# The causal mask moved into PSUM, and the last transform folded twice, in a gated mix of attention and a spectral filter

## The chip, the cores and the metric

The kernel runs on one core of a Trainium2 chip. The metric is the device time of one execution in microseconds. The profiles show one execution each: TensorE (PE, with its weight loads as PEld), VectorE (DVE), ScalarE (ACT), GpSimd (POOL) and the DMA queue of SyncE (SPq).

## What is computed

Input x has 2048 tokens of width 640, in bf16. The output is `g * a + (1 - g) * b`, where g is a sigmoid of one number per token.

```python
# a: attention in 4 segments of 512 tokens, 32 heads of 20
logits = einsum('bhqd,bhkd->bhqk', qs, ks) * scale + mask   # causal inside the segment
a_dot = einsum('bhqk,bhkd->bhqd', softmax(logits), vs)
a_mem = (phi(qs) @ M) / (phi(qs) @ z + 1e-6)                # memory of the segments before
o = gh * a_mem + (1 - gh) * a_dot                           # gh: one gate a head
M, z = M + phi(ks).T @ vs, z + sum(phi(ks))
a = o @ wo
# b: a filter in the frequencies of tokens and width
b = irfft2(rfft2(x) * (w_r + 1j * w_i))
```

## The kernel before, in words

**An order by hand.** The kernel records some 2200 operations, each with the buffers that it reads and writes, and `schedule` (L113) emits them in the order of a list written out in the source, `ORDER` (L741). Each number of that list names an operation and, by its last bit, one of the engines that may run it: a copy out of PSUM goes to ACT or DVE, an addition in SBUF to DVE or POOL. Every engine and SyncE's DMA queue work their share in that order, so an operation can wait for a buffer while those behind it wait too.

**Tile modes of TensorE.** A product with a `tile_position` uses a part of the array, and parts work side by side. The code numbers the modes: 0 is the whole array, 1 the score products (four groups of 32 rows, one for each of four heads, by 64 or 128 columns), 2 four strips of 32 columns, 4 two strips of 64 columns. The order decides how often the mode changes. Nearly all products are issued from L548 in `mms` (L532); the strips into which a projection of the output is cut are issued from L546. Copies out of PSUM are L557 (ACT) and L559 (DVE).

**Attention.** Heads go in 8 groups of four. `project` (L1129) makes q and k, transposed, and v for one segment. `token_order` (L1173) reads the keys' tokens in another order than the queries', with two products of 256 columns for each product of a k tile, and `v_part` (L1327) makes the odd v tiles with their halves swapped, in two strips of 64 columns. `qk_unit` (L1470) fills four PSUM banks with the scores of a unit, one bank for each of the four heads, and ACT takes the exponential into `ex` (L1508). Only the blocks on and under the diagonal are computed, and the 64-wide halves of the diagonal blocks are packed. A unit of kind 0 or 1 has 512 columns in each bank; kind 2 holds the 128 columns that are left of a group, for two groups together (256 columns in each bank). The list `PIECES` (L608) says what lies where. All units use the same four banks, so the next one begins when the exponential has read the last. In the last segment the pieces lie differently in `ex`, and kinds 1 and 2 take two exponentials each.

After the exponential, `masks` and `mask` (L1517, L1533) put zeros above the diagonal: four masks for each group, each either on POOL (selects at L1540 and L1549) or on DVE (a minimum with a table in `hm`, L1539 and L1545). Then `pv_flipped` (L1407) multiplies with v in four strips of 32 columns (five pieces of 512, 64, 320, 256 and 128 columns for each head), or, in the last segment, `pv_group` (L1556) uses the scores as weights on the whole array, ten products of 21 columns for each head.

**The filter.** `fft` (L1632) goes through F1 (over 128 token residues), D (over the width), T and the multiplication with W (L1696, DVE), Tb back, and Db, the back transform over the width: for each of 16 residues n2 and for the cosine and the sine part it adds three products of 321 columns, and ACT or DVE copies the sum to `G`. Db can begin when all of Tb is done.

**The end.** `finish_tile` (L1773) makes the output in 16 tiles of 128 tokens, in two halves of 320 columns. Fb multiplies G with the gated table `fbg` (for the right half's sine part with its negative `fbn`, made at L1249): for the cosine and the sine part each a product of 320 columns in four strips, the right half reading G backwards. Five projection products with wo are added in the same bank, the result is copied to `ot` and stored. The buffers of this stage (`gbc`, `fbg`, `ot`, `oU`, `mT`, `fbn`, `gw3`) lie over those of T and W, and `after_mid` (L968) makes each of them wait for all of these.

Of the kernel before, what the change touches and what calls it, by code (L numbers as in the profile page):

```python
# [322 lines left out]
def make_tables():  # L323
# [34 lines left out]
    ang = 2 * pi * kd[:, None] * kd[None] / D  # L358
    order = np.concatenate([od, [KD], ev])
    inv = np.zeros((2, 384, 322))  # L360
    for n_, (t, zero) in enumerate(((np.cos(ang), ()), (np.sin(ang), (0, 320)))):
        t = ck[:, None] * t
        t[list(zero)] = 0
        inv[n_, :322, :KD] = np.concatenate([t, np.zeros((1, KD))])[order]
    inv[1, :, 320] = 0
    inv = inv.reshape(6, 128, 322).transpose(1, 0, 2).reshape(128, 6 * 322)
# [32 lines left out]
    fcat = np.concatenate([F, np.eye(128), Fp], 1)  # L399
# [5 lines left out]
    p, c = np.arange(128)[:, None], np.arange(64)[None]  # L405
    q = p % 64
    keep = [np.where(t, 3.38e38, 0.0) for t in ((c >= q) & (p >= 64), (c >= q) & (p < 64), (c >= q) | (p < 64), (c >= q) | (p >= 64))]
    m = np.arange(128)[None]
    spread = [1.0 * ((p % 4 == t) & (p // 4 == m // 4)) for t in range(4)]
    hmask = np.concatenate([hmask.reshape(128, 880)] + keep + spread, 1)  # L410
# [80 lines left out]
KPOS = (0, 256, 128, 384)  # L491
VPIECES = ((0, 0, 512, 0), (1, 512, 64, 128), (1, 896, 320, 192), (2, 640, 256, 256), (3, 1216, 128, 384))
# [3 lines left out]
class Kern:  # L496
# [79 lines left out]
    def dma(self, dst, src, nbytes, r, w, prio, tr=False, name="", after=(), queue="sp"):  # L576
        def f(e):
# [3 lines left out]
            with self.nc.allow_non_contiguous_dma(reason="small strided loads"):  # L581
# [9 lines left out]
        "ld_fcat": (400.0, 350.0, 16), "ld_g": (400.0, 1500.0, 16), "ld_gc": (580.0, 200.0, 16), "ld_gw": (420.0, 600.0, 16),  # L591
# [6 lines left out]
        ("xT", 393216): (1400.0, 2600.0, 16), ("xT", 655360): (2950.0, 2100.0, 16)}  # L598
# [8 lines left out]
    UNITS = (((0,), 0), ((0,), 1), ((1,), 0), ((0, 1), 2), ((1,), 1))  # L607
    PIECES = (((0, 0, 0, 0, 0, 512), (1, 64, 64, 128, 0, 64), (0, 64, 64, 64, 64, 448)),  # L608
# [278 lines left out]
    def alloc(self):  # L887
# [25 lines left out]
        def TL(name, shape, dtype=BF):  # L913

            t = T(name, shape, dtype, at=late[0])
            late[0] += (shape[1] * mybir.dt.size(dtype) + 63) // 64 * 64
            assert late[0] <= self.cur
            return t
# [956 lines left out]
```

## Time and profile before

| | |
|---|---|
| median of three runs | 242.66 us (242.34 to 242.94) |
| the profiled execution | 242.17 us, of which the span of its instructions is 240.4 us |
| granted TensorE clock | 1.00 |
| masks on POOL | 110 instructions, 56.2 us |
| DMA | 43.46 MB, 73.9% of the engines' time in the main queue |

Matmuls are pipelined and the end of one is modelled, so TensorE's pace is read from the starts of two neighbours, not from a mean duration. A timeline row gives start, length, engine, line, operation, shapes and a count; neighbours of a like form are merged in one row. A group row ends in busy microseconds and the mean nanoseconds of one.

### The profile page before, as it was taken

The page shows a single profiled execution, that of the slowest core. Times are in us where ns is not written, and L with a number is a line of the kernel's source. Part 1 is how long each engine was busy: PE and PEld are TensorE (multiplying, and loading weights), DVE is VectorE, ACT ScalarE, POOL GpSimd, SP SyncE. Part 2 cuts the span into 40 slices and gives each one's busy share as a digit, 9 for nine tenths or more (in the row PEclk, how much of TensorE's full clock was granted, in tenths as well). Part 3 has the DMA queues.
Part 4 walks back from the last instruction along what each step waited for, and adds up shares of the span by engine and source line. Part 5 has one row for each costly group of instructions (what it writes and reads, how often), then busy time and mean ns, then how long its engine had stood idle before and what let it go on. Part 6 is the DMA issues. An engine that isn't in the chain of part 4 may idle for free.

```text
span 240.4 us, 10161 instructions
## 1 busy us (share of the span) xinstructions
PE 228.9 (95%) x4361; PEld 146.3 (61%) x4361; DVE 203.8 (85%) x493; ACT 202.7 (84%) x253; POOL 92.9 (39%) x172
## 2 busy tenths in 40 slices
PE   7999799999999999999989999999999999999993
PEld 4666367666556674654656555565555667667883
DVE  0978888999999899999999999899999679747742
ACT  2398979999999999999999999899899977678630
POOL 5203415503655407250516733504546232272810
PEclk9999999999999999999999999999999999999999
DMA  7998988678979989849986748378759862782213
GB/s 195 373 182 264 198 270 176 148 239 211 213 146 241 221 215 226 200 136 154 216 246 162 229 129 223 92 197 201 197 154 223 209 151 79 105 90 92 77 43 108
DMA packets 58072, 43.46 MB, mean 181 GB/s; under 512 B 27628, under 2 KB 55724, under 8 KB 58028
## 3 DMA queue, kind: packets, MB, share of 16 engines
q1 hardware_dynamic: 57500, 42.46, 73.9%
q8 instruction: 34, 0.56, 1.0%
q10 hardware_dynamic: 528, 0.36, 0.5%
q14 instruction: 10, 0.08, 0.1%
HBM read 22.73 MB, written 12.20 MB: 145 GB/s over the span
## 4 chain that ended last, share of the span: by engine, by line
PE 60%; DVE 15%; ACT 12%; DMA 6%; SPq 3%; issue 3%; DVEq 0%
PE psum L548 53%; ACT ex L1508 9%; PE psum L546 7%; DMA hm<-tab_hmask 3%; DMA qk_scr<-qu 2%; SPq L582 2%; DMA u_scr<-ub 2%; DVE mem L1389 1%; DVE G L559 1%; DVE oU L1791 1%; DVE ub L559 1%; DVE ex L1545 1%; DVE Pt L1696 1%; ACT qu L557 1%; DVE dn L1381 1%
## 5 line engine op out<-in xcount | busy, mean ns | idle before, releaser
L1508 ACT ACTIVATE ex<-psum 128x2048 bf16<-128x2048 f32 (+4 forms) x92 | 138.6, 1507 | 12.2 <-PE psum L548 10.7
L1549 POOL TENSOR_SCALAR_AFFINE_SELECT ex<-ex 64x256 bf16<-64x256 bf16 x66 | 26.8, 427 | 64.3 <-ACT ex L1508 63.5
L1540 POOL TENSOR_SCALAR_AFFINE_SELECT ex<-ex 128x512 bf16<-128x512 bf16 x44 | 29.4, 678 | 31.7 <-DVE ex L1545 20.3
L548 PE MATMUL psum<-qkp 20*64 20x64 bf16 (+5 forms) x1024 | 31.4, 266 | 1.6 <-ACT ex L1508 0.9
L548 PE MATMUL psum<-wv,xT 128*64 128x320 bf16 (+3 forms) x240 | 26.6, 302 | 2.4 <-DMA wv<-in_A_wv_dram 1.5
L548 PE MATMUL psum<-xT,wk 128*128 128x256 bf16 (+1 forms) x280 | 28.3, 273 | 0.0
L548 PE MATMUL psum<-xT,wq 128*128 128x512 bf16 (+1 forms) x135 | 27.9, 380 | 0.0
L1696 DVE TENSOR_TENSOR Pt<-psum,Wt 128x644 bf16<-128x644 f32 x32 | 25.8, 820 | 1.4 <-PE psum L548 1.1
L548 PEld LDWEIGHTS psum<-xT,wk 128*128 128x128 bf16 (+1 forms) x280 | 20.9, 98 | 4.4 <-issue 0.4
L548 PEld LDWEIGHTS psum<-qkp 20*64 20x64 bf16 (+1 forms) x1024 | 12.1, 100 | 18.1 <-ACT ex L1508 10.9
L546 PE MATMUL psum<-wo,oU 128*32 128x320 bf16 x480 | 21.0, 299 | 0.0
L548 PEld LDWEIGHTS psum<-wv,xT 128*64 128x64 bf16 (+1 forms) x240 | 14.8, 105 | 9.4 <-DMA wv<-in_A_wv_dram 1.7
L559 DVE CAST ot<-psum 128x320 bf16<-128x320 f32 x20 | 9.4, 489 | 10.3 <-PE psum L546 4.5
L548 PE MATMUL psum<-ex,va 128*32 128x512 bf16 (+4 forms) x480 | 17.3, 274 | 0.1
L548 PE MATMUL psum<-big,Cp 128*128 128x321 bf16 (+1 forms) x96 | 16.7, 302 | 0.7 <-DVE rs L1587 0.3
L548 PE MATMUL psum<-tt,Pt 128*128 128x128 bf16 (+1 forms) x192 | 16.4, 221 | 0.0
L1298 ACT ACTIVATE et<-qu 128x512 bf16<-128x512 bf16 x25 | 15.6, 629 | 0.4 <-DVE phk L1311 0.4
L546 PEld LDWEIGHTS psum<-wo,oU 128*32 128x32 bf16 x480 | 12.8, 97 | 3.8 <-issue 0.6
L548 PE MATMUL psum<-big,Ac 128*32 128x160 bf16 (+2 forms) x384 | 14.4, 259 | 0.7 <-DVE mem L1385 0.5
L1545 DVE TENSOR_TENSOR ex<-ex,hm 128x512 bf16<-128x512 bf16 (+1 forms) x31 | 13.8, 453 | 1.3 <-ACT ex L1508 1.0
L548 PEld LDWEIGHTS psum<-tt,Pt 128*128 128x128 bf16 (+1 forms) x192 | 12.1, 102 | 4.4 <-issue 0.9
L548 PEld LDWEIGHTS psum<-xT,wq 128*128 128x128 bf16 (+1 forms) x135 | 9.2, 97 | 8.5 <-issue 1.8
(114 smaller groups left out, 420.6 us busy)
## 6 DMA issues: line engine op xcount, KB each, us to landing
qkp<-qk_scr SPq DMA_DIRECT2D x28, 160.0 KB
qk_scr<-qu SPq DMA_DIRECT2D x12, 256.0 KB, 3.6
tt<-tab_tt SPq DMA_DIRECT2D x8, 384.0 KB, 4.4
u_scr<-ub SPq DMA_DIRECT2D x12, 256.0 KB, 3.6
Wt<-Wt SPq DMA_DIRECT2D x8, 321.0 KB, 4.0
xsb<-in_A_x_dram SPq DMA_DIRECT2D x8, 320.0 KB, 5.4
oU<-u_scr SPq DMA_DIRECT2D x15, 128.0 KB, 3.2
out_dram<-ot SPq DMA_DIRECT2D x12, 160.0 KB
```

The source lines that it names most:

```text
L546: h = e.matmul(dst, wt, r_, start=st, stop=sp_, **{**kw, "tile_position": (0, q), "skip_group_check": True})
L548: h = e.matmul(o_, l_, r_, start=st, stop=sp_, **kw)
L557: alts["act"] = (lambda e: e.activation(dst(), src(), ACT.Copy), 65 + 0.833 * n, 110.0)
L559: alts["dve"] = (lambda e: e.tensor_copy(dst(), src()), 67 + 1.04 * n, 68.0)
L582: return e.dma_start(d_, s_)
L1298: self.one("act", lambda e: e.activation(et.ap(0, [1, L]), qsl(), ACT.Exp), L, [qb], [b("et", pi_)], late, fix=94, name="phi_exp")
L1381: self.one("dve", lambda e: e.reciprocal(dn.ap(32, [1, 32]), dn.ap(0, [1, 32])), 32, [b("dn", i % 2, q) for q in range(2)], [rb], prio, fi ...
L1508: self.one("act", lambda e, d=d, q=q: e.activation(self.ex.ap(*d), self.ps(bank, *q), ACT.Exp, scale=SC), n, [bank], [self.exb(s, 2 * pr + ...
L1540: pick = lambda e: e.affine_select(ex(), ex(), [[0, 4], [1, P]], ALU.is_ge, 0.0, base=0, channel_multiplier=-1)
L1545: least = lambda e: e.tensor_tensor(dst(), src(), self.hm.ap(880 + 64 * t, [0, 4], [0, 2], [1, 64], np_=nd), ALU.min)
L1549: h = e.affine_select(self.ex.ap(e0 + d, [1280, 4], [1, 64], p0=hp, np_=np_), self.ex.ap(e0 + q, [1280, 4], [1, 64], p0=hp, np_=np_), [[0, ...
L1696: self.one("dve", lambda e, x=x, Pt=Pt, Wt=Wt, wo_=wo_, bank=bank: e.tensor_tensor(Pt.ap(x * 644, [322, 2], [161, 2], [1, 161]), self.ps(b ...
```

## The change

- **Scores.** q and k have the same token order. Small products are added into the scores' PSUM after the score products of a unit: weights are a 32-row table U (values -1 and -2^-50), the moving side is a table V (32 rows, 64 columns, values 2^64 and 2^14, read again for each block), so that a large negative number stands above the diagonal before the exponential. A unit of kind 0 gets 8 such products (for each head 64 columns on PSUM partitions 0 to 63 and 128 on 64 to 127), a unit of kind 1 gets 4 (128 columns), a unit of kind 2 gets 8 (256 columns on the first 64 partitions and 512 on the others). All masks go, on POOL and DVE.
- **Units of kind 2** hold four groups (512 columns in each bank) and have a buffer `exc` of their own, used by all groups in turn. Every exponential has 128x2048, in the last segment too: 72 in place of 92.
- **v.** The odd tiles are made on the whole array. New half-zeroed copies `vz` of v, made by `v_half` (16 copies on DVE or POOL for the four segments), serve the packed diagonal halves. `pv_flipped` has eight pieces (three more of 64 columns), the columns together as before; `pv_group` has two products of 64 weight columns, side by side, for each one of 128.
- **Back transform over d.** Odd and even frequencies are kept apart and only d from 0 to 160 is computed: products of 322, 161 and 161 columns in place of three of 321. The cosine part is copied to f32 (`eo`), the sum and the difference with the sine part are made from PSUM (`sum_Db`, 32 on DVE), and two folds for each n2 make the rows of G (`fold_Db`: 21 on POOL, 11 on DVE by the new list). Fb reads 161 and 159 columns where it read 320 and 320, and `fbn` is gone.
- **Homes.** The late buffers lie over other tiles and each waits, once, for the tile that it lies on (`once` in place of `after_mid`).
- **Tables.** `fcat` grows from 64 KB (without the identity) to 128 KB and is loaded earlier, sixth in SyncE's list; the first score unit needs it. `big` and `hm` shrink. The q and k rows of the middle tile are stored with one DMA in place of two.
- **Order.** `ORDER` and `ENDED` are written anew, with 2084 operations in place of 2232.

```diff
-KPOS = (0, 256, 128, 384)
-VPIECES = ((0, 0, 512, 0), (1, 512, 64, 128), (1, 896, 320, 192), (2, 640, 256, 256), (3, 1216, 128, 384))
+KPOS = (0, 128, 256, 384)
+VPIECES = ((4, 0, 64, 0), (0, 64, 448, 64), (5, 0, 64, 128), (1, 832, 320, 192), (2, 640, 192, 320), (6, 576, 64, 256), (7, 576, 64, 384), (3, 512, 64, 448))
...
+    CAUSAL = (((64, 0, 0, 1, 64), (64, 64, 0, 2, 64)),
+              ((0, 0, 0, 2, 192),),
+              ((64, 64, 0, 8, 64), (64, 0, 64, 4, 128)))
...
+        for u0, p0, o, n, step in self.CAUSAL[kind]:
+            for hh in range(4):
+                def th(hh=hh, u0=u0, p0=p0, o=o, n=n, step=step):
+                    return (self.ps(bank, hh * 512 + o, [step, n], [1, 64], p0=p0, np_=m), self.fcat.ap(256 + u0, [1, m], p0=32 * hh, np_=32),
+                            self.fcat.ap(448, [0, n], [1, 64], p0=32 * hh, np_=32), False, True, {"tile_position": (32 * hh, p0), "skip_group_check": True})
...
-        if u == 3:
-            self.masks(s, 2 * pr, prio)
-        elif u == 4:
-            self.masks(s, 2 * pr + 1, prio)
...
+                        for q in (0, 2):
+                            def th(i=i, hh=hh, jj=jj, q=q, bank=bank):
+                                w, v = weights(hh, 4 * i + q, jj)
+                                return (self.ps(bank, i * 88 + hh * VW, [1, DH + 1], p0=32 * q, np_=64), w,
...
+                        kc, n, o, c0 = ((P, 161, 0, 161), (P, 322, 161, 0), (66, 161, 483, 0))[c]
...
+                for q in range(2):
+                    self.one("dve", lambda e, q=q, bank=bank, eo=eo, uv=uv: e.tensor_tensor(
+                        uv.ap(322 * q, [1, 322]), eo.ap(0, [1, 322]), self.ps(bank, 0, [1, 322]), ALU.subtract if q else ALU.add),
...
-                        rows = self.G.ap(o + 322 * n_ + 320 * hf, [1 - 2 * hf, 320])
-                        wt = (self.fbn[s % 3] if hf and n_ else fb).ap(32 * (4 * a + q), [1, 32])
+                        rows = self.G.ap(o + (0, 322)[hf], [1, 161]) if n_ == 0 else self.G.ap(o + (483, 161)[hf] + 159, [-1, 159])
```

More of the change, by code (lines that the diff above doesn't have):

```diff
@@ L1391, in mem_read_tile @@
                     dn.ap(32 + 16 * q, [1, 16], [0, DH]), ALU.mult)
-            self.one("dve", fn, 320, [bank, rb], [b("mem", i, q)], prio, name="mem_mul", after=[b("xf", 2)] if s == 1 else ())
+            self.one("dve", fn, 320, [bank, rb], [b("mem", i, q)], prio, name="mem_mul", after=[b("q0", 8 + x) for x in range(2)] if s == 1 else ())
     def attend(self, s):
@@ L1482, in qk_unit, with th @@
             rb += [b("qp", pidx, j, gl) for j in range(4)] + [b("kp", pidx, j, gl) for j in range(4)]
[L1483 removed]
+            for j, kc, p0, q0, o, n in self.PIECES[kind]:
+                first = p0 not in begun
+                begun.add(p0)
                 for hh in range(4):
[L1485 to L1486 removed]
+                    def th(hh=hh, j=j, kc=kc, p0=p0, q0=q0, o=o + n_ * width, n=n, gl=gl, pad=pad, first=first):
```

350 lines of the change are left out of this document (175 added, 175 removed), and 487 rows, old and new, of tables (ENDED, ORDER, PIECES).

## The prediction, made blind

> **What bounds the kernel now.** I read the page's busy times first, then the windows, the chain, and TensorE's timeline.
>
> ```profile
> PE 228.9 (95%) x4361; PEld 146.3 (61%) x4361; DVE 203.8 (85%) x493; ACT 202.7 (84%) x253; POOL 92.9 (39%) x172
> ...
> PE 60%; DVE 15%; ACT 12%; DMA 6%; SPq 3%; issue 3%; DVEq 0%
> ```
> ```profile
> 40.00:160.00 120.00, 117.32 (x2122) 71.60 (x2115) 113.70 (x269) 115.53 (x136) 49.87 (x100) 1.00 0.80 191
> 160.00:207.00 47.00, 44.94 (x948) 28.16 (x945) 42.22 (x113) 41.11 (x52) 18.56 (x30) 1.00 0.70 169
> 207.00:240.40 33.40, 29.83 (x880) 23.27 (x878) 18.87 (x42) 18.12 (x23) 11.70 (x20) 1.00 0.40 85
> ```
>
> The columns of a window are TensorE, weight loads, VectorE, ScalarE, GpSimd, clock, DMA. From 40 to 160 us three engines are full at once: TensorE 98%, VectorE 95%, ScalarE 96%. Behind 160 TensorE stays at 93% while the other two thin out; GpSimd is never near full. The chain that ended last runs on TensorE for 60% of the span. So a saving on TensorE counts nearly in full, and one on another engine counts where TensorE waits for it. The sum below is TensorE's, against the profiled execution of 242.17 us (span 240.4); it lies 0.49 under the median of the runs.
>
> **Prices on TensorE**, from starts of neighbours in its timeline:
>
> ```profile
> 78.02 0.72 PE L548 MATMUL psum<-ex,va 128*32 128x512 bf16 x20
> 78.67 0.31 PE L548 MATMUL psum<-Bt,tt 128*128 128x322 bf16 x1
> 78.81 1.25 PE L548 MATMUL psum<-xT,wk 128*128 128x256 bf16 x10
> ...
> 80.00 0.47 PE L548 MATMUL psum<-big,Ac 128*32 128x322 bf16 x12
> ...
> 86.25 0.40 PE L548 MATMUL psum<-qkp 20*128 20x192 bf16 x8
> 86.57 0.41 PE L548 MATMUL psum<-tt,Pt 128*66 128x128 bf16 x4
> ...
> 88.68 0.32 PE L548 MATMUL psum<-qkp 20*64 20x64 bf16 x24
> 88.93 1.56 PE L548 MATMUL psum<-wv,xT 128*64 128x321 bf16 x20
> ...
> 92.46 1.24 PE L548 MATMUL psum<-xT,wq 128*128 128x512 bf16 x5
> 93.54 0.30 PE L548 MATMUL psum<-Bt,tt 128*128 128x322 bf16 x1
> 93.77 0.43 PE L548 MATMUL psum<-qkp 20*64 20x512 bf16 x12
> 94.13 0.72 PE L548 MATMUL psum<-wv,xT 128*128 128x321 bf16 x4
> ```
> ```profile
> 188.57 0.32 PE L548 MATMUL psum<-G,fbg 128*32 128x320 bf16 x4
> 188.72 0.31 PE L548 MATMUL psum<-G,fbn 128*32 128x320 bf16 x4
> 188.85 0.45 PE L548 MATMUL psum<-G,fbg 128*32 128x320 bf16 x8
> ...
> 191.12 1.16 PE L548 MATMUL psum<-va,ex 128*128 128x21 bf16 x40
> 192.21 0.32 PE L546 MATMUL psum<-wo,oU 128*32 128x320 bf16 x4
> ```
>
> *A column*: five products of 512 start at 92.46 and the next at 93.54, so 0.216 us each, 0.42 ns a column. *A change of tile mode*: a product of 322 columns takes 0.14 us in front of one of its own mode (78.67 to 78.81) and 0.23 in front of a score unit (93.54 to 93.77), so 0.09; a kind-1 unit takes 0.32 (86.25 to 86.57) for 512 columns in each of its tiles, so 0.11 on leaving. I take 0.10. *Side by side*: the kind-2 unit has 24 products, 2048 columns together; one behind the other these are 0.86 us, and the next product starts after 0.25, a mode change in it. So the tiles do run beside each other, and what counts is the longest tile's columns. The four products of Fb (188.57 to 188.72 to 188.85) take 0.14 us together, the pace of one.
>
> **The terms**, in us of TensorE.
>
> *Db*: per part 644 columns in place of 963, 319 x 0.42 ns = 0.134, 32 parts: -4.3. *Fb*: 320 columns in place of 640 for each of 32 halves, again 0.134: -4.3. Both are streamed on the whole array or in four strips, where the rows above hold the pace, so the bounds are narrow (-3.5 to -4.4 each).
>
> *Mode changes*: walking down TensorE's share of the two lists, neighbours differ in mode 238 times before and 211 times after (fewer score units, no odd v tiles in strips): 27 x 0.10 = -2.7; -2.4 to -3.0.
>
> *The mask's products*: a kind-0 or kind-1 unit gets 128 more columns in its longest tile, 0.054 us; 64 such units, +3.4. Kind 2: the longest tile has 512 score and 512 mask columns, once for four groups, where two units of 256 stood: 512 x 0.42 ns = 0.215 more, 8 times, +1.7. Together +5.1. Products with 32 rows and such a repeated moving side stand nowhere in the trace. The lower bound is 4, if part of it falls into time that a unit loses at its edges; the upper, if nothing ran side by side, is 8192 columns, 3.4 us, for each of 8 times four groups, so 27. The kind-2 row is the nearest thing, with the same tiles, and it is far on the cheap side.
>
> *PV*: 20 products took 0.65 us, less a mode change 0.55, for 1280 columns (0.53): five steps cost 0.02 beyond their columns. Three more steps in 24 groups: +0.3; nothing to +1.5. *PV of the last segment*: 40 products in 192.21 - 191.12 - 0.10 = 0.99 us, 25 ns each. Afterwards each is a pair with half the weights in two strips. If the strips work side by side a pair costs what one did; if not, twice: 0 to +8. I take +0.6, near the cheap end because of the kind-2 row, whose 24 weight loads of 64 columns fit into 0.25 us. *Keys' projection*: ten products of 256 columns take 1.19 us (78.81 to 80.00) with a mode change, so 0.109 each and 0.218 a pair, against 0.216 for one of 512: 100 pairs, -0.3. v's odd tiles keep their columns: 0.
>
> Sum: -4.3 - 4.3 - 2.7 + 5.1 + 0.3 + 0.6 - 0.3 = -5.6.
>
> [...]
>
> **The other engines** must not become the bound.
>
> ```profile
> L1508 ACT ACTIVATE ex<-psum 128x2048 bf16<-128x2048 f32 (+4 forms) x92 | 138.6, 1507 | 12.2 <-PE psum L548 10.7
> L1549 POOL TENSOR_SCALAR_AFFINE_SELECT ex<-ex 64x256 bf16<-64x256 bf16 x66 | 26.8, 427 | 64.3 <-ACT ex L1508 63.5
> L1540 POOL TENSOR_SCALAR_AFFINE_SELECT ex<-ex 128x512 bf16<-128x512 bf16 x44 | 29.4, 678 | 31.7 <-DVE ex L1545 20.3
> ```
> ```profile
> L1508 ACT ACTIVATE ex<-psum 128x2048 bf16<-128x2048 f32 x56 | 105.2, 1878 | 6.9 <-PE psum L548 6.2
> ...
> L1539 DVE TENSOR_TENSOR ex<-ex,hm 128x512 bf16<-128x512 bf16 x20 | 10.7, 544 | 2.0 <-ACT ex L1508 1.9
> ...
> L559 DVE CAST G<-psum 128x321 bf16<-128x321 f32 x18 | 8.4, 485 | 0.3 <-PE psum L548 0.3
> ...
> L1545 DVE TENSOR_TENSOR ex<-ex,hm 128x512 bf16<-128x512 bf16 x19 | 8.0, 422 | 1.3 <-ACT ex L1508 1.0 <-DMA hm<-tab_hmask 0.3
> ...
> L1385 DVE TENSOR_TENSOR mem<-psum,dn 128x320 bf16<-128x320 f32 x16 | 7.2, 484 | 0.2
> ...
> L1545 DVE TENSOR_TENSOR ex<-ex,hm 64x512 bf16<-64x512 bf16 x12 | 6.0, 503 | 0.0
> ...
> L1597 POOL TENSOR_TENSOR on<-on,mem 128x320 bf16<-128x320 bf16 x6 | 4.8, 808 | 6.9 <-DVE on L1592 6.9
> ```
>
> ScalarE: 72 x 1.878 = 135.2 in place of 138.6, and by the lists 94 copies in place of 105, at about 0.5 each: -9. VectorE: masks -24.7 (10.7 + 8.0 + 6.0); 150 copies in place of 155, -2.5; 32 `sum_Db` of 322 f32 from PSUM, near L1385's 0.484, +15.5; 11 folds, between 0.42 and 0.48 by the rows of two SBUF inputs, +5; 12 `v_half`, no dearer than these, +4; so about -3, and -1 to -6 with the small ones. GpSimd: masks -56, 21 folds at some 0.8 to 1, +19. All loads fall. But VectorE's relief lies ahead of 160 us, and the sums and folds lie in the stage of Db, where it had 42.2 of 47 us; there it loses 7.3 of masks (the third busy time of the row below, which is the same stretch for the instructions on `ex` alone) and, with 8 copies fewer, 4, and gains 20.
>
> ```profile
> 160.00:207.00 47.00, 7.71 (x240) 6.07 (x240) 7.33 (x19) 33.06 (x28) 10.61 (x21) 1.00 0.70 169
> ```
>
> The new list spreads Db further out, beside Fb and the projection, so that TensorE has work while VectorE sums; that is the cover, and without it the stage would wait for VectorE (rival 2).
>
> *Waits.* `exc` is one buffer for all groups: the kind-2 exponential waits for PV of the four groups before, and ScalarE's next copies stand behind it. The new list puts those PVs right ahead of that score unit; I cost it at nothing, at most half a microsecond, seven times. `vz` is single too: `v_half` waits for the last PV of the segment before and VectorE's copies stand behind it; nothing, to +1. The table for the mask's products is 128 KB and moved past eight loads in SyncE's list; the first score unit now needs it, and the x and weight loads stand behind it: nothing, as TensorE projects until then, to +1. The late loads wait for one tile each and can only start earlier.
>
> The forecast is 242.17 - 5.6 = **236.6 us**; its own range, with the narrow bounds and the waits, 233.5 to 239.8.
>
> **Rivals.**
>
> 1. *The waits shrink too.* ScalarE idled 10.7 us ahead of exponentials for scores and TensorE waited in turn; with 20 exponentials fewer and no masks between exponential and PV, some 5 us of that may go: 231 to 232. For it: three engines full from 40 to 160. Against: all units still share four banks, so score and exponential alternate as before. 0.17.
>
> 2. *VectorE becomes the bound in the stage of Db, slower than before.* Place: from the last Tb to the last G. The added sums and folds are 20 us there at the prices above, and a fold on GpSimd beside one on VectorE can lengthen both.
>
> ```profile
> 214.89 1.73 DVE L1539 TENSOR_TENSOR ex<-ex,hm 128x512 bf16<-128x512 bf16 x1 [1.95 <-ACT ex L1508]
> ```
>
> This minimum, 0.544 on average, took 1.73 while GpSimd selected. If a sum or a fold costs 0.8 in place of 0.48, 43 of them add 14 us, of which the spread list hides perhaps half; +7 leaves 243.6, and up to 247. It decides from about 0.75 a piece, where the stage eats the 5.6. Against: sums read one side from PSUM, like L1385, which is steady. 0.12. [...]
>
> 3. *Half-width weights double the last PV.* +8 in place of +0.6, on TensorE behind 190 us, where it is the bound: 244. It decides from a pair of about 44 ns, where the gain is gone.
>
> ```profile
> L548 PEld LDWEIGHTS psum<-va,ex 128*128 128x128 bf16 x320 | 8.8, 96 | 1.0 <-DVE ot L559 0.3 <-issue 0.3
> ...
> L548 PEld LDWEIGHTS psum<-wv,xT 128*64 128x64 bf16 x160 | 8.1, 109 | 3.8 <-DVE qu L559 0.8 <-issue 0.7 <-ACT et L1298 0.3
> ```
>
> For it: a load of half the columns is shown as longer, 109 ns against 96, and it never stood before so few moving columns. Against: the kind-2 row. 0.06.
>
> 4. *The gain goes into new waits* for `exc`, `vz` or the late loads (+3 to +5.5, all bounds at once): 240 to 242.2. 0.10.
>
> **Numbers.** Forecast 0.55, rivals 0.17, 0.12, 0.06, 0.10. About 0.3% is what a measurement of this kernel can tell from none, here 241.9 to 243.4. Faster: 0.55 + 0.17 + most of rival 4, 0.08 = 0.80; same: the rest of it and a little of 2 and 3, 0.05; slower 0.15. The range takes in rival 1 and rival 4 and leaves out most of 2 and 3: 230.5 to 242.5.
>
> **What would show it.** TensorE: Db's products in steps of 0.07 and 0.14, four of Fb in 0.07; a kind-1 unit 0.37 to its follower, a kind-2 unit 0.55; 80 products of the last PV in about 1.05. Group rows: exponentials x72 near 1878 ns, sums near 485, GpSimd under 60 us. By the windows the work up to the last Tb ends about where it did (mask +3.3, mode changes -2.8 there), and the gain appears behind it. Wrong would be: mask products behind one another (a kind-1 unit of 0.5 or more), or VectorE full from the last Tb on with TensorE waiting for `sum_Db`.

## The result and the profile after

The changed kernel takes **267.2 us** (four runs, 263.0 to 270.7) where the kernel before takes 242.56 (242.3 to 242.9): slower by a factor of 1.087 (95% interval 1.082 to 1.093). That factor goes by the two fast runs of the change, 263.0 and 264.6, and the profiled run is one of the two slow ones. I had forecast 236.6 and a range up to 242.5.

The page of the profiled execution (269.83 us, span 268.0): busy times, the granted clock in 40 slices, the queue that brings TensorE's instructions, the chain.

```profile
PE 238.0 (89%) x5304; PEld 150.0 (56%) x5325; DVE 200.2 (75%) x480; ACT 195.5 (73%) x214; POOL 64.6 (24%) x91
...
PEclk9999999995999999999999999986999658979979
...
q8 instruction: 42, 0.69, 1.1%
...
PE 54%; DMA 19%; DVE 11%; issue 5%; ACT 5%; SPq 3%; POOL 1%; DVEq 0%
```

VectorE, ScalarE and GpSimd have less to do, as forecast, yet TensorE is busy for 89% of a longer span (95% before), the clock falls to 0.5 in places, and DMA holds 19% of the chain (6% before). The waits of TensorE, first of the kernel before, then of the change (total, times, longest):

```profile
PE psum L548 <- DMA wv<-in_A_wv_dram: 1.5, 1, 1.5
...
PE psum L548 <- issue: 0.4, 1, 0.4
```
```profile
PE psum L553 <- issue: 7.8, 9, 2.1
PE psum L553 <- DVE qu L564: 5.9, 4, 3.2
PE psum L553 <- DVE mem L1400: 2.3, 1, 2.3
```

"issue" is a wait for which the profile names no releaser. One of the nine is a wait for data all the same:

```profile
99.03 0.70 SPq L587 DMA_DIRECT2D qkp<-qk_scr  x1
...
105.12 0.40 PE L553 MATMUL psum<-qkp 20*128 20x192 bf16 x8 [2.10 <-issue]
```

TensorE's sequencer stands from 102.65 to 105.07 at the semaphore of that load of score operands, and the last part of the load lands at 105.03. The same wait, of 1.6 to 2.5 us, stands at 100 to 107 us in the traces of runs 1 to 3, 9 to 12, 14 and 16. Without it the waits with no releaser come to 5.7 us in the change.

**The account.** From the profiled executions: the time in which a product or a weight load of TensorE is on record (busy), the rest (idle), and the busy time that lies in stretches at half clock, of which half is taken off to get the work at full clock.

| us | span | idle | busy at half clock | work at full clock |
|---|---|---|---|---|
| before | 240.4 | 11.4 | 0 | 229.1 |
| change | 268.0 | 29.2 | 32.4 | 222.7 |
| difference | +27.6 | +17.8 | +16.2 for its half | -6.4 |

So the work did shrink. Everything else is waits and clock. The last column is rough, since the ends of products are modelled: runs 9 and 14, with the same products as the change, come out at 227.8 and 224.8. And the clock's part differs between executions: by their mean granted clocks (0.936 here; 0.961, 0.949 and 0.948) half clock takes 17 us of this one and 10 to 14 us of the other three.

**The work's prices.** TensorE's timeline of the change: eight products of Fb, a unit of kind 1 with its mask, then the last segment's PV.

```profile
204.91 0.32 PE L553 MATMUL psum<-G,fbg 128*32 128x161 bf16 x8
205.06 0.85 PE L551 MATMUL psum<-wo,oU 128*32 128x320 bf16 x20
...
206.18 0.40 PE L553 MATMUL psum<-qkp 20*128 20x192 bf16 x8
206.41 0.23 PE L553 MATMUL psum<-fcat 32*128 32x128 bf16 x4
206.56 0.20 PE L553 MATMUL psum<-vz,ex 128*64 128x21 bf16 x1
...
207.90 0.17 PE L553 MATMUL psum<-va,ex 128*64 128x21 bf16 x1 [0.41 <-issue]
210.19 0.23 PE L553 MATMUL psum<-va,ex 128*64 128x21 bf16 x3 [2.11 <-issue]
```
```profile
96.73 0.71 PE L553 MATMUL psum<-qkp 20*64 20x64 bf16 x64
97.25 0.40 PE L553 MATMUL psum<-fcat 32*64 32x512 bf16 x8
97.59 0.31 PE L553 MATMUL psum<-Bt,tt 128*128 128x322 bf16 x1
```

Eight products of Fb take 0.15 (0.07 for four), the kind-1 unit 0.38 to its follower: as forecast. The kind-2 unit takes 0.86, not 0.55. And between 207.90 and 210.19 TensorE stands for 2.1 us in the middle of one PV, at a product that waits for no semaphore.

**The clock.** Windows of 3.41 us, in pairs: one that ends where the clock drops, and the one after (length, busy us and count of TensorE, loads, VectorE, ScalarE, GpSimd, clock, DMA).

```profile
25.53:28.94 3.41, 1.68 (x29) 0.80 (x29) 1.13 (x3) 2.84 (x3) 0.06 (x1) 1.00 0.41 106
56.25:59.66 3.41, 1.30 (x41) 0.95 (x39) 0.00 (x0) 2.08 (x4) 0.00 (x0) 1.00 1.21 219
59.66:63.07 3.41, 2.29 (x104) 1.59 (x104) 2.76 (x9) 0.60 (x1) 0.74 (x3) 0.50 0.86 100
175.71:179.13 3.42, 1.07 (x24) 0.57 (x25) 1.30 (x5) 1.62 (x1) 1.16 (x2) 1.00 0.84 204
179.13:182.54 3.41, 3.08 (x77) 1.89 (x65) 2.94 (x10) 1.85 (x2) 1.70 (x3) 0.50 1.09 240
206.43:209.85 3.42, 1.23 (x60) 0.97 (x50) 1.82 (x5) 2.55 (x3) 0.00 (x0) 1.00 0.54 124
209.85:213.26 3.41, 3.07 (x83) 2.39 (x82) 1.34 (x5) 0.00 (x0) 0.00 (x0) 0.50 0.26 55
...
250.81:254.22 3.41, 2.21 (x133) 2.04 (x131) 2.14 (x7) 0.00 (x0) 0.79 (x1) 1.00 0.16 48
254.22:257.63 3.41, 3.41 (x54) 2.90 (x52) 1.21 (x3) 0.13 (x1) 0.00 (x0) 0.50 0.12 40
```

The clock changes on a grid of 3.413 us. Five stretches run at 0.5: 59.66 to 66.49, 179.13 to 185.95, 209.85 to 223.50, 237.15 to 240.57 and 254.22 to 257.63, together 34.1 us; before there was none up to the last microsecond. Each follows a window in which TensorE was busy for 1.1 to 1.3 us, or a little over 2 where the products were small and dense (133 in the last case). A window with 1.68 busy of big products (the first row) drops nothing.

Idle time is not the whole rule. Run 10 has a window in which TensorE never pauses, full of products of 21 columns in the last PV, and the clock halves behind it:

```profile
243.43:246.84 3.41, 3.41 (x116) 2.86 (x104) 1.26 (x5) 0.74 (x1) 0.00 (x0) 1.00 0.20 73
246.84:250.25 3.41, 3.41 (x68) 2.23 (x65) 2.14 (x7) 0.00 (x0) 0.79 (x1) 0.50 0.18 53
```

An estimate from the shapes in the traces fits both kinds of window: for each product its columns at 0.42 ns, times the share of the array's 128 rows and of its 128 columns that it uses, summed over a window. Call this the use of the array. In the 18 traces here there are 1238 windows at full clock. All 65 with a use under 1.13 us, a third of the window, have half clock behind them; of the 20 between 1.13 and 1.25, 8 do; of the 1153 above, none. The five windows of the change have 0.99, 0.65, 0.25, 0.61 and 0.60, the first row above 1.22, the one of run 10 0.88. The lowest of the kernel before in its trace is 1.42. So a stall and a row of small products pull in the same direction.

**Where a stall comes from.** The chain of the change from 50 to 70 us (start, length, what):

```profile
52.43 0.61 DVE qu L564
...
53.36 6.49 DMA qk_scr<-qu
...
59.94 0.70 DVE qu L564
...
60.77 2.23 PE psum L553 x90
```

VectorE writes `qu`, the store of it needs 6.5 us among loads of W, tt and the table `big`, and VectorE's next copy into the same buffer waits for that store; PV, a score unit and other products of TensorE stand behind it. TensorE waits 3.2 us, and the clock is at half for 6.8 us from 59.66 on.

The longest of the waits without a releaser, but for the load of `qkp` above, lie beside fetches of instructions. The queue of row q8 brings 16 KB at a time, 42 times for 10629 products and loads (34 times before). Its records in the trace, with the instructions of TensorE that started since the fetch before:

```
fetch, us            since the one before    wait of TensorE
207.58 to 208.73     392                     208.07 to 210.19
233.01 to 234.17     386                     234.08 to 235.46
251.79 to 252.71     355                     252.92 to 254.12
```

The mean is 253. Where small products ran close together, some 100 more had started before the next fetch began, and TensorE stood until 1.3 to 1.5 us after it had landed. The count alone does not decide: in the same trace 413, 388 and 359 had started before the fetches at 64.31, 167.18 and 128.19, and no wait of this kind stands there.

### The profile page after: what moved, and what is told of

Its sections match the earlier page's. It is cut to its first block, busy times and chain, and to the rows that moved or that the text cites. A ratio compares the mean times of both kernels' runs of the same rounds, so it can differ in the third digit from the quotient of the medians.

```text
span 268.0 us, 11905 instructions
## 1 busy us (share of the span) xinstructions
PE 238.0 (89%) x5304; PEld 150.0 (56%) x5325; DVE 200.2 (75%) x480; ACT 195.5 (73%) x214; POOL 64.6 (24%) x91
## 4 chain that ended last, share of the span: by engine, by line
PE 54%; DMA 19%; DVE 11%; issue 5%; ACT 5%; SPq 3%; POOL 1%; DVEq 0%
PE psum L553 47%; PE psum L551 7%; DMA qk_scr<-qu 5%; DMA o_scr<-mem 3%; SPq L587 3%; DMA qk_scr<-q 3%; ACT ex L1525 2%; DMA Wt<-in_B_w_r_dram 2%; DMA wv<-in_A_wv_dram 2%; DMA qkp<-qk_scr 2%; DMA u_scr<-ub 2%; DVE UV L1716 1%; DMA Wt<-Wt 1%; DVE oU L1781 1%; DVE Cp L564 1%
## 5 line engine op out<-in xcount | busy, mean ns | idle before, releaser
L1525 ACT ACTIVATE ex<-psum 128x2048 bf16<-128x2048 f32 x64 | 120.2, 1878 | 21.0 <-PE psum L553 20.0
L553 PE MATMUL psum<-qkp 20*64 20x64 bf16 (+4 forms) x1152 | 33.2, 266 | 3.1 <-issue 2.1
L553 PE MATMUL psum<-wv,xT 128*128 128x320 bf16 (+1 forms) x160 | 29.0, 308 | 1.2 <-DMA wv<-in_A_wv_dram 1.2
L553 PE MATMUL psum<-xT,wk 128*128 128x512 bf16 (+1 forms) x129 | 25.9, 379 | 1.4 <-issue 0.5
L553 PE MATMUL psum<-fcat 32*64 32x128 bf16 (+4 forms) x448 | 19.4, 236 | 1.4 <-issue 1.4
L1525 ACT ACTIVATE exc<-psum 128x2048 bf16<-128x2048 f32 x8 | 15.0, 1877 | 7.2 <-PE psum L553 7.1
L1720 POOL TENSOR_TENSOR G<-UV 128x322 bf16<-128x322 f32 x21 | 16.6, 804 | 12.7 <-DVE UV L1716 11.7
L553 PEld LDWEIGHTS psum<-wv,xT 128*128 128x128 bf16 x160 | 14.6, 100 | 8.6 <-ACT Ac L562 1.3
L1603 POOL TENSOR_TENSOR Mz<-Macc,hm 128x154 bf16<-128x154 f32 (+1 forms) x15 | 7.6, 508 | 36.3 <-DVE Macc L1601 22.6
L1716 DVE TENSOR_TENSOR UV<-eo,psum 128x322 f32<-128x322 f32 x32 | 15.4, 483 | 1.2 <-PE psum L553 0.7
L553 PE MATMUL psum<-ex,va 128*32 128x192 bf16 (+2 forms) x288 | 16.1, 322 | 0.0
```

Source lines behind the costliest of these rows:

```text
L553: h = e.matmul(o_, l_, r_, start=st, stop=sp_, **kw)
L1525: self.one("act", lambda e: e.activation(d(), self.ps(bank, 0, *q), ACT.Exp, scale=SC), 2048, [bank], [self.exb(s, 4 * qd + gp, "abc"[kind ...
L1603: self.one("pool", lambda e, o=o, w=w: e.tensor_tensor(self.Mz[nb].ap(o, [1, w]), self.Macc.ap(o, [1, w]), self.hm.ap(o, [1, w]), ALU.mult ...
L1716: self.one("dve", lambda e, q=q, bank=bank, eo=eo, uv=uv: e.tensor_tensor(uv.ap(322 * q, [1, 322]), eo.ap(0, [1, 322]), self.ps(bank, 0, [ ...
L1720: fn = lambda e, q=q, n2=n2, uv=uv: e.tensor_tensor(self.G.ap(n2 * 644 + 322 * q, [161, 2], [1, 161]), uv.ap(0, [322, 2], [1, 161]), uv.ap ...
```

## Theories and experiments

*Supply:* the added products (448 for masks, 320 for the halved PV weights) use up instructions faster than they come. *Waits:* the new list leaves too little time between a transfer and its use. *Clock:* either kind of stall costs about as much again, since the clock halves behind it. Rivals: the added products simply cost more than their columns; the clock is an accident of the execution. A difference of some 4 us from the change's 267.2 says little, as its own four runs lie between 263.0 and 270.7. Times are medians of four runs (six for the half fold) beside runs of the kernel before on the same chip, whose medians lay between 241.9 and 242.8.

**1. No mask products.**

```diff
-    CAUSAL = (((64, 0, 0, 1, 64), (64, 64, 0, 2, 64)),
-              ((0, 0, 0, 2, 192),),
-              ((64, 64, 0, 8, 64), (64, 0, 64, 4, 128)))
+    CAUSAL = ((), (), ())
```

> The changed kernel without the mask's small products (448 products fewer; the causal mask is left out). Theory supply (TensorE runs out of instructions where small products stand close together, and each such stall lets the granted clock drop): these products cost more than their columns; the stall at 234 us and the half clock behind it go, no stretch between fetches with 350 and more TensorE instructions there; 250 to 258 us. Rival waits (the new order's transfers and buffers cost the time, the products only their columns): 267 - 5 = 262 us, the stalls at 27, 57 and 176 us as before.

265.5 us (264.1 to 266.4). Supply is wrong for this part: the unit of kind 1 falls from 0.387 to 0.329 us as it should, work and stalls stay (issue 10.1 us, 7.6 of them without the wait for `qkp`), and the saving goes unseen. The mask's products are not the loss.

**2. Whole weights in the last PV**, one product of 128 weight columns in place of a pair.

```diff
-                        for q in (0, 2):
-                            def th(i=i, hh=hh, jj=jj, q=q, bank=bank):
-                                w, v = weights(hh, 4 * i + q, jj)
+                        def th(i=i, hh=hh, jj=jj, bank=bank):
+                            w, v = weights(hh, 4 * i, jj)
```

> The changed kernel with the last segment's PV as whole 128-column weights, one product for each pair (320 products fewer; the blocks on the diagonal are multiplied from the wrong places). Supply: the 2 us stall inside that PV and the 13.7 us of half clock behind it go, 253 to 259 us. Rival waits: the pair cost about what the single one did, 267 - 1 = 266 us, with half-clock stretches as many as before.

258.2 us (253.0 to 260.3). As supply expected: -9. The issue waits fall from 7.8 to 4.0 us (without the wait for `qkp`, from 5.7 to 1.9), idle from 29.2 to 22.6, busy at half clock from 32.4 to 16.8. This run does not part two reasons for the half clock, the stall inside PV and the pairs themselves: 21 columns are 8.8 ns of use, 27% of the 32 ns that a pair takes in run 4 and 35% of the 25 ns of a whole product, below and at the bound of 33 to 37% of a window above.

**3. Both.**

> Both of the edits before: no mask products (mask left out) and the last PV on whole weights (wrong blocks on the diagonal). Supply: 768 products and six instruction fetches fewer, stalls without a releaser back to the 0.4 us of before, 243 to 250 us; what is left over 231 is the transfers' stalls. Rival waits: 267 - 6 = 261 us.

257.3 us (253.3 to 258.0), where supply had 243 to 250: run 2 over again, a second time nothing for the masks. The last PV's pairs stand at a third of the loss.

**4. The kernel before with pairs in the last PV**, its only change:

```diff
-                        def th(i=i, hh=hh, jj=jj, bank=bank):
+                        for q in (0, 64):
+                            def th(i=i, hh=hh, jj=jj, q=q, bank=bank):
...
+                                        {"tile_position": (0, q), "skip_group_check": True})
```

> The kernel before, with nothing but the last segment's PV cut into pairs of 64 weight columns, side by side (320 products more, same result). My prediction's price: +0.6 and mode changes, 243.5 us. Half-width weights cost double: 250 us. Supply: 640 TensorE instructions more in the stage behind 185 us, where fetches already follow each other every 4 us: a stall of 1 to 2 us inside PV and a drop of the clock behind it, 246 to 254 us.

250.3 us; factor 1.028 (1.020 to 1.037). TensorE's timeline and the window after:

```profile
190.09 1.44 PE L548 MATMUL psum<-va,ex 128*64 128x21 bf16 x80
191.46 0.31 PE L546 MATMUL psum<-wo,oU 128*32 128x320 bf16 x1
193.51 0.32 PE L546 MATMUL psum<-wo,oU 128*32 128x320 bf16 x3 [1.74 <-issue]
```
```profile
193.82:197.23 3.41, 3.41 (x62) 1.68 (x55) 0.34 (x2) 1.88 (x1) 0.08 (x1) 0.50 0.67 177
```

40 pairs take 1.37 less a change of mode, 32 ns a pair where a whole product took 25: +2.2 us for 320, not the +8 of double cost. The rest is a stall and the clock: 483 instructions started before the fetch at 191.15, TensorE stands for 1.74 us, and half clock follows. In the account of this run work is +2.6, idle +1.8, half clock +1.7.

**5 and 6. The order of the kernel before**, carried over operation by operation, with the change's PV and with whole weights.

> All parts of the change, same result, but the order of the kernel before: its list is taken over operation by operation on every engine and queue; only what is new (v_half, the sums and folds) is put in as soon as its inputs are there, and what the one exc buffer forbids comes later. Theory order (the new list's transfers and buffers come too late, that is 12 to 15 us of stalls and the half clock behind them): the stalls at 27, 57 and 176 us go, what is left is the dense last PV, 243 to 252 us. Rival supply alone: the list does not matter, 262 to 268 us. Rival parts (single exc and vz make waits in any order): also 260 or more, with TensorE waiting for copies into qu, exc or vz.

> As the run before, and the last PV on whole 128-column weights (wrong blocks on the diagonal). If order and the dense PV are the two causes, what is left of the change is my forecast's sum without its PV term: 236 us, at most 243 with some clock lost. If the parts themselves (masks in PSUM, exc, sums) carry a cost that I missed, 250 or more.

412.8 and 410.0 us. These tell nothing on the question. Where one `exc` serves four groups, my carried-over list made TensorE wait for exponentials (36.6 us), for operands of the scores (28.6 us) and for sums (10.0 us). An order fits its operations; this one wasn't a fair copy. What the new list costs as a whole stays open. (One of the seven runs of the kernel before beside these two and run 7 took 410.2 us at full clock. It has no trace, and nothing here explains it.)

**7. Pauses in the kernel before**, four reductions of 2.84 us each on VectorE ahead of multiplications with W.

```diff
+                def pause(e, x=x, g=g, bank=bank):
+                    if x and g in (4, 7, 10, 13):
+                        e.tensor_reduce(self.idle.ap(g // 3 - 1, [1, 1]), self.ps(bank, 0, [0, 8], [1, 322]), op=ALU.max, axis=mybir.AxisListType.XY)
+                    return e
```

> The kernel before with four pauses: a reduction of 8 x 322 f32 from PSUM, some 2.7 us, stands on VectorE ahead of four of the multiplications with W, same result. Theory clock (an idle stretch of TensorE of 1.4 us or more halves its granted clock for the 3.4 us that follow, or longer): rows of 0.5 behind the pauses that reach TensorE, and more time than the pauses' own 10.9 us, 253 to 262 us. Rival: the clock stays 1.00 and the time grows by the part of 10.9 us that reaches TensorE, 246 to 253 us.

The four runs took 252.1, 252.1, 258.3 and 259.2 us, at mean clocks of 0.986, 0.993, 0.959 and 0.966. It is the same program, and the lower clocks account for the difference: by them half clock takes 3.5, 1.8, 10.5 and 8.8 us. In the profiled one (252.1) the pauses reach TensorE as idle stretches of 2.2, 2.5, 2.3 and 2.5 us, and only the second halves the clock. Two of them in windows of the grid:

```profile
108.76:112.17 3.41, 1.04 (x5) 0.31 (x4) 3.41 (x3) 1.64 (x1) 1.22 (x3) 1.00 0.78 221
112.17:115.58 3.41, 3.25 (x40) 1.73 (x41) 2.29 (x8) 1.89 (x2) 0.40 (x1) 0.50 1.07 156
...
153.13:156.54 3.41, 1.76 (x28) 0.77 (x20) 3.31 (x3) 2.55 (x3) 1.16 (x3) 1.00 0.82 259
156.54:159.96 3.42, 2.55 (x64) 1.64 (x64) 3.42 (x9) 1.49 (x1) 0.00 (x0) 1.00 0.73 205
```

A pause of which 2.4 us lie inside one window (1.04 busy, use 0.85) drops the clock, one as long that is spread over two (1.76 and 2.55 busy, use 1.26 and 1.79) doesn't. So the clock follows what TensorE does, but whether a given stall triggers it depends on where the grid falls, as far as this trace shows. That the change scatters by 8 us for that reason is likely and not shown, since one of its runs alone has a trace.

**8. The full fold alone**, in the kernel before and its order: the edits of Db and Fb of the change (the last three parts of its diff), `UV` where `fbn` was, `eo` over the first x buffer.

> The kernel before with the back transform over d folded twice as its only change, same result: attention, masks, late buffers and the order of everything else as before; a sum stands where VectorE's copy of that part of Db stood, a fold a few entries behind it, 21 on GpSimd and 11 on VectorE. If the prices are all that counts: TensorE -8.6 us, 234 to 237 us, clock 1.00, since the order keeps its slack. Rival (my rival 2, VectorE becomes the bound between the last Tb and the last G, where it was busy for 42 of 47 us): the added 20 us of VectorE show, 241 to 248 us, TensorE waiting for the sums.

260.4 us; factor 1.075 (1.068 to 1.082). Worse than my rival had it. Waits of TensorE, and the windows of the stage:

```profile
PE psum L551 <- DVE UV L1741: 4.4, 4, 1.7
PE psum L551 <- ACT eo L560: 2.8, 3, 1.7
```
```profile
165.94:179.59 13.65, 11.67 (x134) 6.41 (x138) 13.32 (x31) 6.33 (x7) 10.17 (x16) 0.50 0.46 124
...
186.42:206.90 20.48, 15.31 (x173) 7.05 (x177) 18.20 (x36) 10.17 (x11) 12.53 (x17) 0.50 0.29 89
```

VectorE is full (13.3 of 13.7 us), TensorE waits for `UV` and `eo`, and with little to do between the waits it stays at half clock for 41 us in all. In the account of this run the work is -9.5 us, near the forecast's -8.6 for Db and Fb; idle +11.1 and half clock +16.5 outweigh it.

**9. Lighter transfers**, from the third pair on, 37.9 MB in place of 43.4:

```diff
+        m = 32 if pair < 2 else 4
...
-                    src = lambda wd=wd, row=row, pitch=pitch, gap=gap, n=n: dap(wd, row * KD, [pitch * KD, 32], [gap * KD, n], [1, KD])
+                    src = lambda wd=wd, row=row, pitch=pitch, gap=gap, n=n: dap(wd, row * KD, [pitch * KD, m], [gap * KD, n], [1, KD])
```

> The changed kernel with lighter transfers in the same order: from the third pair on the loads of W, their copy and the loads of tt bring 1/8 of their partitions, some 5.4 MB of 43 less (the filter is computed from stale tables). Theory waits (data transfers that land late because others stand ahead of them): the waits behind 90 us, at 176 and 188 us above all, and the half clock behind the first go, 257 to 263 us. Rival (these waits come from the order of copies on VectorE and ScalarE, not from the transfers): 264 to 270 us with the same gaps.

261.0 us (257.4 to 264.2, which touches the change's range). As waits expected: -6; TensorE's wait for `mem` falls from 2.3 to 0.2 us, the stall at 176 us is gone with its half clock; the stalls inside PV stay (issue 7.9 us).

**10. Pairs on the diagonal only.**

```diff
+                    for jj in range(i):
+                        def th(i=i, hh=hh, jj=jj, bank=bank):
+                            w, v = weights(hh, 4 * i, jj, P)
...
+                    for q in (0, 2):
+                        def th(i=i, hh=hh, q=q, bank=bank):
+                            w, v = weights(hh, 4 * i + q, i, 64)
```

> The changed kernel with pairs of 64-column weights only where they are needed, on the diagonal blocks of the last segment's PV; the blocks under it go as whole weights (192 products fewer, same result). Supply: the stalls inside that PV shrink and with them the half clock, 256 to 262 us, between the change and the run with whole weights (258). Rival waits: 266 us or more, since each of the 32 ops now changes the tile mode inside (+3 us).

261.3 us (256.9 to 262.7; unlike expected, that PV adds up other sums here, with the count and the shapes of products as said). Between the two, as supply expected; issue waits 3.9 us, 2.0 of them without the wait for `qkp`.

**11. Projection on whole weights** (L545).

```diff
-                if op.mode < 0 and op.emode == 2:
+                if False:
```

> The changed kernel with the projections of the first three segments' output as whole products where the list had them cut into four strips (360 products and as many weight loads fewer, in the stretches around the last PV; same result; same columns, but each change between Fb's strips and a whole product costs 0.1, some 5 us in all). PV and masks are untouched. Supply: the next instructions are there in time more often, so TensorE's waits with no releaser inside PV and the products beside it fall from 7.8 us to under half, and the half clock behind them with it; 255 to 264 us. Rival (the stalls belong to the half-width PV itself): the same stalls, 270 to 273 us.

260.5 us; factor 1.076 (1.063 to 1.089). PV and masks untouched, 720 instructions fewer near them:

```profile
PE psum L553 <- issue: 4.5, 9, 1.8
```

From 7.8 to 4.5, a little over half; without the loads of `qkp`, from 5.7 to 2.5, under half. Half clock goes from 34.1 to 3.4 us. With PV as it was, stalls and half clock shrink, so they belong to what else stands in the stretch as well, the count of instructions above all. Part of the gain is paid back (work +6 us against the change in the rough account; more changes of mode, at the 0.1 us read from the trace of before, would do that).

**12. Both causes off**, whole weights and light transfers.

> The changed kernel with both suspected causes off: the last PV on whole weights (wrong blocks on the diagonal) and from the third pair on W, its copy and tt with 1/8 of their partitions (stale tables). Masks, exc, vz, sums and folds as in the change. If supply and late transfers carry the loss and add up: 267 - 9 - 6 = 252 us, the rest in the stalls ahead of 65 us, which these edits don't reach, with gaps of TensorE near 13 us and half clock under 15 us. If something else in the parts takes it up again: 256 us or more, with other gaps in their place.

250.1 us (248.4 to 253.0), 252 expected: the two add up. Idle 21.2 us, where 13 had been expected; half clock 6.8 us.

**13. Half the fold** in the kernel before.

```diff
+                for q in range(2):
+                    self.one("dve", lambda e, q=q, bank=bank, eo=eo, n2=n2: e.tensor_tensor(
+                        self.G.ap(n2 * 644 + q * 322, [1, KD]), eo.ap(0, [1, KD]), self.ps(bank, 0, [1, KD]), ALU.subtract if q else ALU.add),
...
+                            self.G.ap((4 * a + q) * 644 + 642 * hf, [1 - 2 * hf, 320]), True, False,
```

> The kernel before with half of the folding, same result: Db keeps its three products of 321 columns; the cosine part is copied to f32 by ScalarE and VectorE writes the sum and the difference with the sine part straight into G (32 sums, no folds), so Fb needs 4 products of 320 columns for each half where it took 8; the rest of the list as before. TensorE -4.3 us. VectorE gets 32 sums of 0.48 for 18 copies of 0.48, +7 us, in a stage where it is busy 42 of 47 us. If the full fold was slow because VectorE could not follow, this one follows: 238 to 241 us with the clock at 1.00. Rival (any pair of copy and sum behind one another makes TensorE wait, as with the full fold): 244 to 252 us with half clock.

250.8 us (six runs); factor 1.034 (1.027 to 1.041). The rival: even a third of the load on VectorE makes TensorE wait.

```profile
PE psum L548 <- DVE G L1734: 2.8, 5, 1.4
PE psum L548 <- ACT eo L557: 2.1, 3, 1.7
```

Between 160 and 210 us VectorE is busy for 43.1 of 50 us, so it isn't full. What is left is the chain of product, copy on ScalarE, product and sum on VectorE, with a list that was written for two independent copies; no run here loosens that chain, so this cause is argued.

**14 to 16. The x loads.** In the change the loads of x ahead of the stores of q and k (14); the mirror of that in the kernel before (15); and the first on top of run 12 (16). SyncE's entries, by name:

```diff
-xT(1) x(5) store store store store gw x(6) x(4)
+x(5) x(6) x(4) xT(1) store store store store gw
```

> The changed kernel with one edit of SyncE's list: the last three loads of x stand ahead of the transposed load and of the four stores of q and k, as in the kernel before. Theory waits: VectorE's fold of x no longer waits 3.7 us at 24 us with the copy of qu behind it, and TensorE's stall of 2.1 us at 27 us goes: 2 to 5 us less than the change, 262 to 265 us. Rival: the stores land later by as much and TensorE waits for the scores' operands in its place: 267 us.

> The kernel before with the mirror of that edit: two loads of x stand behind the four stores of q and k, as in the change. Theory waits: VectorE waits for them, the copies that TensorE waits for stand behind, a stall of 1 to 3 us between 22 and 32 us, with half clock behind it where it fills most of one clock window: 244 to 248 us. Rival (the list has slack enough): 242.5 us, no new gap.

> The run with whole weights in the last PV and light transfers (250 us), and the x loads early. If the three causes add: 250 - 2 to 4 = 246 to 248 us and no stall at 28 us. If not: 250 us and another wait in its place.

Run 15, the mirror: 245.8 us, factor 1.015 (1.009 to 1.022), with one new stall and one window of half clock for it.

```profile
32.49 1.93 PE L548 MATMUL psum<-wv,xT 128*64 128x321 bf16 x18 [2.11 <-ACT va L557]
```
```profile
29.85:33.26 3.41, 1.30 (x20) 0.83 (x18) 3.34 (x10) 1.28 (x3) 1.66 (x2) 1.00 1.13 318
33.26:36.67 3.41, 3.41 (x25) 1.96 (x22) 3.38 (x12) 2.17 (x7) 1.19 (x2) 0.50 0.84 275
```

2.1 of stall and 1.7 for half clock make 3.8, and 3.3 are measured, as waits expected: one place in SyncE's list is enough. But in the change the edit moves the wait rather than taking it away: 265.1 us (run 14), and 252.6 in place of 250.1 on top of run 12 (run 16), with

```profile
PE psum L553 <- DMA wv<-in_A_wv_dram: 3.5, 1, 3.5
```

in run 14, and 4.3 for the same load in run 16, in place of the 2.1 for `qu`. The rival's kind of result holds there: where one load comes in time another is late.

## Why the prediction was wrong

**The sum on TensorE (-5.6)** had the right sign, and -6.4 by the account, which is rough by some 5 us. Fb and Db came at their price (eight products of Fb in 0.15, six of Db in 0.57), masks of kinds 0 and 1 at 0.057 us for 0.054. Mis-sized: the kind-2 unit, 0.86 for 0.55, because its 64 score products of 64 columns take 8 ns each, more than their columns; 8 units, +2.5. And the pairs of the last PV, +2.2 for +0.6 (run 4). With these two put right the sum is -1.5. Rival 3's place was right and its price of +8 was not; the +7.8 that run 4 measures came by another way. The forecast's own range, 233.5 to 239.8, does not follow from the bounds it names (their low ends add up to 234.1); that changes nothing here.

**The step that failed is the clock and the cover.** "So a saving on TensorE counts nearly in full" took over from the kernel before that TensorE is hardly ever idle and stays at full clock. All its terms are durations of work, and the waits stood at nothing. In their place the runs showed +17.8 us of idle time and +16.2 for half clock against a saving of 6.4.

*Instruction supply* was in no term and no rival. Runs 4, 2 and 11 show it from three sides: products added, taken out, and others nearby taken out. With the pairs' own price and the clock, it is worth 9 of the 25 us (run 2). That the stalls are fetches is read from their place beside them; run 1, with 448 products fewer, keeps its stalls, and why one stretch runs dry and another doesn't stays open.

*Waits, costed at nothing to +1 each.* Those I named were harmless: TensorE never waits for `exc` or `vz` in the list of its waits. Those that came stand at buffers that I hadn't looked at, `qu`, `mem`, wv and `qkp`, where the list stores, loads and reuses with no time to spare. Rival 4, new waits, was the right kind with 0.10, but at other buffers and at most a third of the size. Lighter transfers give back 6 us (run 9); moving one load did not mend the front up to 35 us (runs 14 and 16).

*The clock.* I read 1.00 as a property of the machine; it was one of a kernel with few gaps, and even that one runs at a mean clock of 0.983 to 0.993, a window or two at half, in 15 of its 39 runs beside the experiments. In the profiled run half clock is 16.2 us of the loss. On the grid of 3.413 us a gap of 2.1 us (run 15) and one of 2.4 us inside one window (run 7) were enough to halve it, and run 10 shows half clock behind a window with no gap at all (3.41 us busy of 3.41).

*Rival 2, VectorE as the bound in the stage of Db*, had 0.12. In the order of before VectorE is full there, at +18 us (run 8), though not by dearer sums: they take 0.49 us at the median, and the folds 0.75 on GpSimd and 0.49 on VectorE, as the forecast had them. In the change TensorE waits 1.1 us for `UV` and 0.7 for `eo`: the spread list does cover the sums, as I argued, but by a longer stage: from the first to the last product of Db 54.5 us (175.3 to 229.8), where it was 37.9 (163.1 to 201.0).

*"The work up to the last Tb ends about where it did"* failed outright: the last Tb ends at 174.5 us, not 160.3.

**What stays open.** With both causes off (run 12) the span is still 8.4 us above before: work -4.6, idle +9.8, half clock +3.1. The waits left lie at loads ahead of 65 us, at the load of `qkp` (1.7), in the stage of Db and in 2.7 us without a releaser. How much of that is the new list, and how much would come with any list, isn't shown, since the list couldn't be exchanged (runs 5 and 6). Nor is it shown how much of the half clock behind the last PV comes from its stalls and how much from its small products. No run here beats the kernel before.

## What to carry to other kernels

Where TensorE is busy for 95% at full clock, ask of each change first what gaps it makes and only then what it saves: a stall of 2.1 us that filled most of one clock window of 3.41 us cost 3.3 (run 15). Count instructions beside columns; cutting products into smaller ones that run side by side cost 2.2 us on the array (32 ns for 25) and 3.5 in idle time and half clock (run 4). Keep the use of the array, not only TensorE's busy time, above 1.25 us of each window of 3.41: by the estimate from the shapes no such window had half clock behind it. And a chain of two engines in place of two independent copies needs an order of its own.

## What the runs showed of the hardware

- In the 18 traces the granted clock is 1.0 or 0.5 and changes on a grid of 3.413 us. All windows in which TensorE was busy for 1.41 us or less had half clock behind them; from 1.42 to 3.41 both happened. The use of the array (columns at 0.42 ns, times the share of rows and columns used; an estimate from the shapes) parts them: under 1.13 us all 65 windows dropped, above 1.25 none of 1153. At half clock, with 0.83 ns a column (change: one of 322 columns starts at 65.89 us and the next product at 66.16, 0.27 where it is 0.14 at full clock), all 54 windows with a use of 2.64 us or more were followed by full clock and none of the 107 under 2.30, which is about the same number of columns. So half clock lasted 3.41 us in the best case, 13.65 (change, 209.85) or 20.48 us (run 8) where small products or waits followed. The same program differs by 7 us with its clock (run 7).
- The fetches of row q8 bring 16 KB each and take about 1 us. One came for every 253 products and loads of TensorE in the change (42 for 10629) and for every 257 before (34 for 8722), so they are read as its instructions. Stalls of 1.2 to 2.7 us came where 355 to 483 had started since the fetch before, and one of 1.3 us where 266 had (run 10, 205.79); 413 passed without one in the kernel before and in the change, so the count alone doesn't decide.
- Products with weights of 64 columns over all 128 rows, two strips side by side, took 32 ns a pair with their loads (run 4), where one with weights of 128 columns took 25 (kernel before).
